# Two layers of linear attention and MLP on one core: the first tile's mean is taken ahead of its statistics, and the engines' lists are reordered

## The chip, the core and the metric

The kernel runs on one core of one Trainium2 chip. A core has five engines that run their own instruction streams and meet through semaphores: TensorE (PE in the profile; PEld is its weight load), VectorE (DVE), ScalarE (ACT), GpSimd (POOL) and SyncE (SP), which here only issues DMA transfers. TensorE writes to PSUM, a memory of eight banks; all other data lie in SBUF, 128 partitions wide. The metric is the time of one execution on the device, in microseconds (us). Smaller is better.

## The reference

`x` is 2048 tokens by 512 features in bf16. Four residual blocks follow each other: A, B, A, B, all with the same weights.

```python
def _A_ref(x, wqkv, wo):            # x is already layer-normed; H = 32 heads of 16
    q, k, v = split(x @ wqkv)
    phi = lambda t: jnp.where(t > 0, t + 1, jnp.exp(t)) + 1e-6
    pq, pk = phi(q), phi(k)
    kv = jnp.einsum("bhsd,bhse->bhde", pk, v)
    z = jnp.einsum("bhsd->bhd", pk)
    o = jnp.einsum("bhqd,bhde->bhqe", pq, kv) / (jnp.einsum("bhqd,bhd->bhq", pq, z)[..., None] + 1e-6)
    return merge(o) @ wo

def _B_ref(x, w1, b1, w2, b2):      # a layer norm of its own, 512 -> 1792 -> 512
    y = _layernorm(x)
    return gelu(y @ w1 + b1) @ w2 + b2

x = x + _A_ref(_layernorm(x), A_wqkv, A_wo)
x = x + _B_ref(_layernorm(x), B_w1, B_b1, B_w2, B_b2)     # and both once more
```

## The kernel before

Tokens are cut into 16 tiles of 128 (`st` = 0 to 15) and four chunks of four tiles (`c` = `st // 4`). Layer L (0 or 1) is one A block and one B block. All weights and the residual stay in SBUF.

A block. `norm` (L713) makes a normed tile `y` from `x`: statistics (`stats`, L741) and their aggregate (`aggr`, L743) on VectorE, variance plus epsilon (`veps`), its power -1/2 on GpSimd (`pow`, L756), and then centre and scale in one instruction (`norm`, L781 on VectorE, L776 on ScalarE). The four tiles of chunk 3, which is worked first (`C0=(3, 0, 1, 2)`), go another way: they are only centred (`cen`, L722), turned and projected, and the factor `rstd` is applied in the ScalarE instructions that read the projection (`exp`, `relu`, L848 and L859, with a scale from SBUF). The scaled `y` itself is made later (`ysc`, L766 and L763). A tile is turned (features onto partitions) either by TensorE with an identity matrix (`PT`, L823) and a ScalarE copy (`tc`, L833), or by a DMA transpose from SP (`TA`, `TB`, `TP`). `attn_k` (L869) and `attn_q` (L898) project it: `K0_12` is layer 0, tile 12; `Q0_3_1` is layer 0, chunk 3, tile 1 of the chunk. `phi` (L841) turns a projection into phi(k) or phi(q): `exp` and `relu` on ScalarE, `min` and a sum on VectorE (or GpSimd). `G` (L1004, L1036) sums y^T phi(k), so that v is never formed; `za` (L957) sums phi(k) over tiles; `KV`, `M` and `D` make from these the matrix that `WO` (L1152) multiplies phi(q) with, and its denominators.

B block. `mlp_front` norms and turns a tile (`TB`), `mlp_up` makes 14 groups of four matmuls `W1`L`_`c`_`ft (L1184, for chunk 0 in two halves of two tiles, last index 0 and 1) with a gelu each on ScalarE (L1190), `mlp_down` two groups of seven matmuls per tile (`W2`, last index 0 and 7, L1223), `RA` and `RB` are the residual sums on VectorE, and `b2`L`_`st adds the bias to the residual on VectorE or GpSimd.

Start. SP issues the loads: two tiles of chunk 3 (`x0`), the K and Q weights in two halves by rows (`wk0`, `wk1`), the other two tiles (`x2`), then the other chunks. TensorE runs 16 matmuls on constants (`warm`, L697) until the first tile is there. The first tile alone (`K_SPLIT=1`) is turned in two halves (`PTA0_12_0` and `PTA0_12_1`, L804, copied at L811), and its K and Q projections run in two halves, the first of which needs only `wk0` (L887, L917). `idle0_0` and `idle0_1` are two and one more matmuls on constants (`N_IDLE=[2, 1]`). The weights of V, the output projection and the MLP are loaded by six DMAs that GpSimd issues (`wv`, `wo`, `w1_0`, `w1_1`, `w2_0`, `w2_1`), the biases by SP (`b1`, `b2`).

Order. Nothing is ordered at run time. `CONF["ORDER"]` names for each engine every instruction in the order in which it runs; the program works out from the data which semaphores each has to wait for, and buffers and banks go to tiles as the lists' own estimate of time has them come free. `WAY` says which engine or which variant an instruction takes, `"normA0_5": "act"` for one.

Of the kernel before, what the change touches and what calls it, by code (L numbers as in the profile page):

```python
# [10 lines left out]
P = 128  # L11
# [271 lines left out]
def assign_waits(graph, order, sems, dma_sems):  # L283
# [10 lines left out]
    while len(done) < total:  # L294
        moved = False
        for e in ENGINES:
# [43 lines left out]
    N_WARM2=9, N_IDLE=[2, 1], XQ='sp', WKQ='sp sp', WK1=1, K_SPLIT=1, K_HALVES=(0, 1), X_HEAD=((0, 2), (2, 2)),  # L340
# [39 lines left out]
        "act":  # L380
# [164 lines left out]
def build_kernel(nc, A_x, A_wqkv, A_wo, B_x, B_w1, B_b1, B_w2, B_b2, out, conf=None, report=False):  # L545
# [5 lines left out]
    with ExitStack() as es:  # L551
# [161 lines left out]
        def norm(src, src_keys, src_tiles, double, on_act, prio, tag, src16=False, head=False):  # L713

            s = Tile(STATS, f"st{tag}")
            k = f"st{tag}"
            by_act = eng(f"st{tag}") == "act"
            centred = eng(f"cen{tag}") is not None

            def centre(mean, op):  # L720
                y = Tile(YB, f"y{tag}")
# [698 lines left out]
```

## Time and profile before

| | |
|---|---|
| time, median of 3 runs | 326.31 us (325.96 to 327.42) |
| time of the profiled execution | 326.6 us |
| its span, first to last instruction | 324.9 us |
| TensorE busy | 319.8 us, 98% of the span, 1703 matmuls |
| VectorE, ScalarE, GpSimd busy | 224.4, 193.7, 144.6 us |
| granted TensorE clock | 1.0 throughout |
| first DMA of x landed, first real matmul | 3.5 us, 5.34 us |
| last matmul started | 322.1 us |

The profiled execution is 1.7 us longer than its span, which is what lies ahead of the first and behind the last instruction. In the page, a row names the line, the engine, the operation, what it writes and reads, and the count; the bracket behind a row says how long the engine stood idle before it and what released it. The slices in tenths show how busy an engine was in each fortieth of the span. Ends of matmuls are modelled, so distances between starts are safer than busy times there.

### The profile page before, as it was taken

The page shows a single profiled execution, that of the slowest core. Times are in us where ns is not written, and L with a number is a line of the kernel's source. Part 1 is how long each engine was busy: PE and PEld are TensorE (multiplying, and loading weights), DVE is VectorE, ACT ScalarE, POOL GpSimd, SP SyncE. Part 2 cuts the span into 40 slices and gives each one's busy share as a digit, 9 for nine tenths or more (in the row PEclk, how much of TensorE's full clock was granted, in tenths as well). Part 3 has the DMA queues.
Part 4 walks back from the last instruction along what each step waited for, and adds up shares of the span by engine and source line. Part 5 has one row for each costly group of instructions (what it writes and reads, how often), then busy time and mean ns, then how long its engine had stood idle before and what let it go on. Part 6 is the DMA issues. An engine that isn't in the chain of part 4 may idle for free.

```text
span 324.9 us, 4758 instructions
## 1 busy us (share of the span) xinstructions
PE 319.8 (98%) x1703; PEld 157.9 (49%) x1703; DVE 224.4 (69%) x508; ACT 193.7 (60%) x333; POOL 144.6 (45%) x231
## 2 busy tenths in 40 slices
PE   7999999999999999999999999999999999999996
PEld 3444445567444444444444444558644444444443
DVE  4998979997998854003779999899899666100032
ACT  3999699745253235899527656978934734563300
POOL 4699476646522862500346825755904543100000
PEclk9999999999999999999999999999999999999999
DMA  7343179003331221210110300121230421300012
GB/s 259 144 64 72 40 236 355 18 16 76 40 64 35 58 57 32 43 22 17 34 33 16 67 17 0 18 48 36 41 72 18 82 65 50 81 0 15 31 65 69
DMA packets 46355, 20.37 MB, mean 63 GB/s; under 512 B 42044, under 2 KB 44220, under 8 KB 46332
## 3 DMA queue, kind: packets, MB, share of 16 engines
q1 hardware_dynamic: 45132, 15.32, 20.6%
q0 software_dynamic: 1056, 4.72, 4.1%
q8 instruction: 13, 0.21, 0.3%
q14 instruction: 10, 0.08, 0.1%
q10 hardware_dynamic: 144, 0.03, 0.0%
HBM read 8.00 MB, written 2.10 MB: 31 GB/s over the span
## 4 chain that ended last, share of the span: by engine, by line
PE 88%; DVE 4%; POOL 3%; DMA 2%; issue 1%; ACT 0%; SPq 0%
PE ps L1184 30%; PE ps L1223 29%; PE ps L1152 9%; PE ps L878 5%; PE ps L1036 4%; PE ps L908 4%; PE ps L1004 2%; PE ps L934 2%; DMA t<-in_A_x_dram 2%; DVE stats L741 1%; POOL rstd L756 1%; PE ps L1210 1%; PE ps L1128 1%; POOL zacc L957 1%; DVE yb L781 1%
## 5 line engine op out<-in xcount | busy, mean ns | idle before, releaser
L1190 ACT ACTIVATE gT<-ps,b1c 128x512 bf16<-128x512 f32 (+1 forms) x140 | 76.9, 600 | 70.9 <-PE ps L1184 70.6
L1184 PE MATMUL ps<-t,w 128*128 128x512 bf16 (+1 forms) x560 | 102.6, 336 | 0.0
L1223 PE MATMUL ps<-w,gT 128*128 128x512 bf16 x434 | 98.2, 379 | 0.0
L1184 PEld LDWEIGHTS ps<-t,w 128*128 128x128 bf16 x560 | 54.5, 98 | 43.9 <-ACT t L833 0.6
L1223 PEld LDWEIGHTS ps<-w,gT 128*128 128x128 bf16 x434 | 42.5, 98 | 50.5 <-ACT gT L1190 0.2
L848 ACT ACTIVATE eb<-ps 128x512 bf16<-128x512 f32 x56 | 32.8, 608 | 17.2 <-PE ps L878 10.6
L756 POOL TENSOR_TENSOR rstd<-veps,neghalf 128x1 f32<-128x1 f32 x64 | 38.7, 615 | 5.6 <-DVE veps L754 3.2
L1233 DVE TENSOR_TENSOR pkb<-ps,xsb 128x512 bf16<-128x512 f32 x15 | 10.0, 682 | 32.8 <-PE ps L1223 32.7
L741 DVE BATCH_NORM_STATS2 stats<-xsb 128x6 f32<-128x512 f32 x48 | 32.2, 681 | 0.2
L878 PE MATMUL ps<-wqkv,t 128*128 128x512 bf16 x124 | 31.2, 379 | 0.0
L1229 DVE TENSOR_TENSOR xsb<-ps,xsb 128x512 f32<-128x512 f32 x16 | 10.9, 686 | 29.2 <-PE ps L1223 29.2
L1152 PE MATMUL ps<-gtb,t 128*128 128x512 bf16 x128 | 30.7, 379 | 0.0
L754 POOL TENSOR_SCALAR veps<-mv 128x1 f32<-128x1 f32 x29 | 8.3, 297 | 39.1 <-DVE mv L743 38.4
L859 ACT ACTIVATE rb<-ps 128x512 bf16<-128x512 f32 x38 | 22.7, 612 | 2.0 <-PE ps L878 1.5
L776 ACT ACTIVATE yb<-xsb,nmr,rstd 128x512 bf16<-128x512 f32 x21 | 16.8, 812 | 10.8 <-POOL nmr L773 10.8
L781 DVE TENSOR_SCALAR yb<-xsb,mv,rstd 128x512 bf16<-128x512 f32 x27 | 15.3, 574 | 10.1 <-POOL rstd L756 9.9
L1169 POOL TENSOR_TENSOR xsb<-xsb,b2b 128x512 f32<-128x512 f32 x14 | 17.6, 1258 | 5.4 <-DVE yb L781 4.9
L1116 POOL TENSOR_TENSOR t<-t,rr 128x512 bf16<-128x512 bf16 x7 | 7.7, 1100 | 26.2 <-DVE rr L1112 16.5
L746 POOL TENSOR_SCALAR veps<-mv 128x1 f32<-128x1 f32 x32 | 10.2, 319 | 20.6 <-DVE mv L743 18.8
L1152 PEld LDWEIGHTS ps<-gtb,t 128*128 128x128 bf16 x128 | 12.4, 98 | 14.0
L908 PE MATMUL ps<-wqkv,t 128*128 128x512 bf16 x76 | 19.2, 379 | 0.0
L878 PEld LDWEIGHTS ps<-wqkv,t 128*128 128x128 bf16 x124 | 11.8, 98 | 14.5 <-ACT rb L859 0.6
(102 smaller groups left out, 415.9 us busy)
## 6 DMA issues: line engine op xcount, KB each, us to landing
w<-in_B_w_dram POOLq DMA_DIRECT2D x4, 896.0 KB, 7.2
out_dram<-pkb SPq DMA_DIRECT2D x15, 128.0 KB, 2.0
t<-in_A_x_dram SPq DMA_DIRECT2D x3, 512.0 KB, 7.3
wqkv<-in_A_wqkv_dram SPq DMA_DIRECT2D x2, 512.0 KB, 4.6
t<-yb SPq DMA_TRANSPOSE x56, 2.5
t<-in_A_x_dram SPq DMA_DIRECT2D x2, 256.0 KB, 4.2
wqkv<-in_A_wqkv_dram POOLq DMA_DIRECT2D x1, 512.0 KB, 4.4
wo<-in_A_wo_dram POOLq DMA_DIRECT2D x1, 512.0 KB, 5.1
```

Of the source, the lines that this page charges most:

```text
L741: G.op("dve", lambda e: e.bn_stats(stats[:, s.slot, :], src()), 602, reads=src_keys, writes=[k + "s"], tiles=[s, *src_tiles], prio=prio, n ...
L756: G.op("pool", lambda e: e.tensor_tensor(rstd[:, s.slot:s.slot + 1], veps[:, s.slot:s.slot + 1], neghalf[:], op=ALU.pow), 530, reads=[k + ...
L781: G.op("dve", lambda e: e.tensor_scalar(yb[:, y.slot, :], src(), stats[:, s.slot, 2:3] if by_act else mv[:, s.slot, 0:1], rstd[:, s.slot:s ...
L848: G.op("act", lambda e: e.activation(eb[:, et.slot, :], bank(bt), ACT.Exp, scale=factor()), 569 if by else 483, reads=[src_key, *more], wr ...
L859: G.op("act", lambda e: e.activation(rb[:, rt.slot, :], bank(bt), ACT.Relu, scale=factor()), 569 if by else 478, reads=[src_key, *more], w ...
L878: ins = e.matmul(bank(b), lhsT=yTa(yT)[:, dt, k * P:(k + 1) * P], rhs=wqkv[:, dt, D:2 * D], start=(dt == 0), stop=(dt == DT - 1))
L908: ins = e.matmul(bank(b), lhsT=yTa(yT)[:, dt, k * P:(k + 1) * P], rhs=wqkv[:, dt, 0:D], start=(dt == 0), stop=(dt == DT - 1))
L1152: ins = e.matmul(bank(wb), lhsT=yTa(pq)[:, kt, k * P:(k + 1) * P], rhs=gtb[:, kt, :], start=(kt == 0), stop=(kt == DT - 1))
L1169: G.op("pool" if on_pool else "dve", lambda e: e.tensor_tensor(xsb[:, st, :], xsb[:, st, :], b2b[:], op=ALU.add), 1120 if on_pool else 600 ...
L1184: ins = e.matmul(bank(b, n), lhsT=w1[:, dt, ft * P:(ft + 1) * P], rhs=yTa(yT)[:, dt, k0 * P:k1 * P], start=(dt == 0), stop=(dt == DT - 1))
L1190: G.op("act", lambda e, ft=ft, b=b, k0=k0, k1=k1, n=n: e.activation(gT[:, g.slot, ft * 512 + k0 * P:ft * 512 + k1 * P], bank(b, n), ACT.Ge ...
L1223: ins = e.matmul(bank(b), lhsT=gT[:, g.slot, ft * 512 + k * P:ft * 512 + (k + 1) * P], rhs=w2[:, ft, :], start=(ft == 0), stop=(ft == FT - 1))
```

## The change

Three things are done at the head, and all lists are written anew.

1. The first tile (12) and the second (13) no longer take the mean from `bn_stats`. For tile 12 ScalarE sums the second half of each row (an activation copy with an accumulator) while VectorE sums the first half (`redA0_12`, a reduction); `negA0_12` adds the two and multiplies by -1/512; the tile is centred in two halves (`cenA0_12_1`, then `cenA0_12_0`), and each half of its turn waits only for its half. For tile 13 ScalarE sums the whole row. The statistics follow behind the centring and serve only the variance.
2. `K_SPLIT` is 2: K and Q of tile 13 are projected in two halves too (its turn stays whole). `N_IDLE` is `[4, 1]`.
3. The lists of all five engines are new, over the whole kernel. The instructions themselves, apart from the above, are the same and run on the same engines.

```diff
-    N_WARM2=9, N_IDLE=[2, 1], XQ='sp', WKQ='sp sp', WK1=1, K_SPLIT=1, K_HALVES=(0, 1), X_HEAD=((0, 2), (2, 2)),
+    N_WARM2=9, N_IDLE=[4, 1], XQ='sp', WKQ='sp sp', WK1=1, K_SPLIT=2, K_HALVES=(0, 1), X_HEAD=((0, 2), (2, 2)),
...
         "pe":
-            "warm PTA0_12_0 PTA0_12_1 idle0_0 PTA0_13 idle0_1 K0_12_0 K0_12 Q0_3_0_0 Q0_3_0 K0_13 PTA0_14 Q0_3_1 "
-            "PTA0_15 K0_14 G0_12_0 K0_15 Q0_3_2 Q0_3_3 G0_13_0 PTA0_1 K0_0 G0_14_0 K0_1 G0_15_0 G0_0_0 K0_3 K0_2 "
...
+            "warm PTA0_12_0 PTA0_12_1 idle0_0 Q0_3_0_0 PTA0_13 Q0_3_0 idle0_1 K0_12_0 K0_12 K0_13_0 K0_13 Q0_3_1_0 "
+            "PTA0_14 PTA0_15 Q0_3_1 K0_14 K0_15 Q0_3_3 G0_12_0 Q0_3_2 G0_13_0 K0_0 PTA0_1 G0_14_0 K0_1 K0_3 G0_15_0 "
+            "K0_2 Q0_0_2 G0_0_0 Q0_0_3 Q0_0_0 G0_1_0 K0_8 G0_2_0 K0_4 G0_3_0 K0_6 K0_10 K0_5 Q0_0_1 K0_11 G0_4_0 K0_7 "
...
+            "W10_0_1_0 W10_0_0_0 W10_0_13_0 W10_0_8_0 W10_0_7_0 W10_0_11_0 W20_0_0 W10_0_9_0 W10_0_12_0 W20_1_0 "
+            "W20_1_7 W10_0_13_1 W10_0_7_1 W10_0_1_1 W10_0_6_1 W20_0_7 W10_0_3_1 W10_0_4_1 W10_0_5_1 W10_0_10_1 "
...
+            "W11_3_1_0 W11_3_7_0 W11_3_3_0 W11_3_0_0 W11_3_5_0 W11_3_9_0 W11_3_4_0 W21_5_0 W11_3_11_0 W11_3_6_0 "
+            "W21_5_7 W11_3_13_0 W11_3_10_0 W11_3_2_0 W21_7_7 W11_2_3_0 W11_2_7_0 W11_2_10_0 W11_2_2_0 W21_13_0 "
...
         "act":
-            "tcA0_12_0 tcA0_12_1 tcA0_13 reluk0_12 expk0_12 expq0_3_0 reluq0_3_0 tcA0_14 expk0_13 reluk0_13 tcA0_15 "
+            "sumA0_12 sumA0_13 tcA0_12_0 tcA0_12_1 tcA0_13 expq0_3_0 reluq0_3_0 reluk0_12 expk0_12 tcA0_14 tcA0_15 "
+            "reluk0_13 expk0_13 reluq0_3_1 expk0_14 reluk0_14 normA0_3 expq0_3_3 reluq0_3_3 expq0_3_1 expk0_15 tcA0_1 "
...
+            "gelu1_2_1_0 gelu1_2_6_0 gelu1_2_12_0 gelu1_2_11_0 gelu1_2_0_0 gelu1_2_5_0 gelu1_2_9_0 gelu1_2_13_0 "
...
         "dve":
-            "ones statsA0_12 statsA0_13 aggrA0_12 aggrA0_13 cenA0_12 cenA0_13 vepsA0_12 yscA0_13 yscA0_12 statsA0_14 "
...
+            "ones redA0_12 negA0_12 cenA0_12_1 cenA0_12_0 statsA0_12 negA0_13 aggrA0_12 cenA0_13 vepsA0_12 statsA0_13 "
+            "aggrA0_13 yscA0_12 statsA0_14 statsA0_15 aggrA0_14 aggrA0_15 cenA0_14 cenA0_15 statsA0_0 vepsA0_14 "
...
+            "phiq0_0_3 mink0_8 phiq0_3_0 normA0_11 phik0_8 mink0_4 phik0_4 mink0_6 phiq0_0_2 mink0_10 phik0_10 "
...
+            "cpm0_2 pz0_2_0 red0_2_0 RA0_0 statsB0_0 RA0_1 statsB0_1 aggrB0_0 aggrB0_1 RA0_3 RA0_2 normB0_1 pz0_3_1 "
+            "normB0_0 RA0_4 minq0_2_3 statsB0_3 RA0_5 pz0_3_0 statsB0_2 RA0_6 red0_3_1 aggrB0_2 RA0_7 aggrB0_3 "
+            "statsB0_7 red0_3_0 statsB0_5 minq0_2_2 normB0_2 den0_3_1 normB0_3 red0_3_2 den0_3_2 statsB0_4 minq0_2_1 "
...
+            "RB1_4 statsB1_10 aggrB1_10 normB1_10 b21_11 normB1_8 b21_13 b21_8 RB1_5 RB1_7 RB1_12 RB1_13 RB1_15_0 "
...
         "pool":
-            "powA0_4 nmrA0_7 powA0_9 powA0_6 nmrA0_6 nmrA0_9 za0_0 za0_1 vepsA0_11 powA0_11 za0_2 za0_3 phik0_6 w2_1 "
-            "phiq0_1_2 wv wo phiq0_1_1 w2_0 w1_1 w1_0 pr0_1_0 pr0_0_2 pr0_1_1 pr0_1_2 pr0_1_3 vepsB0_1 powB0_1 "
...
+            "nmrA0_7 vepsA0_11 vepsA0_9 powA0_11 powA0_9 za0_0 nmrA0_9 za0_1 za0_2 phik0_6 za0_3 eps6 phiq0_1_1 "
+            "phiq0_1_2 wo wv w2_0 w1_0 pr0_0_2 pr0_1_0 pr0_1_1 w1_1 w2_1 pr0_1_2 pr0_1_3 vepsB0_1 powB0_1 vepsB0_0 "
+            "powB0_0 phiq0_2_3 b20_0 vepsB0_2 powB0_2 pz0_3_2 vepsB0_3 powB0_3 vepsB0_7 vepsB0_6 vepsB0_5 vepsB0_4 "
...
         "sp":
-            "TB0_1 TB0_2 TB0_3 TP0_3_1 TP0_2_0 TB0_6 TB0_4 TB0_5 TB0_7 TP0_2_3 TP0_2_2 TP0_3_0 TP0_2_1 TP0_3_2 "
+            "TB0_1 b2 TB0_3 TB0_2 TP0_3_0 TP0_3_2 TB0_7 TB0_5 TB0_6 TB0_4 TP0_3_3 TP0_2_0 TP0_2_3 TP0_3_1 TP0_2_2 "
...
+            "TB1_12 TB1_13 TB1_15 OD2 TB1_9 TB1_10 TB1_11 TB1_8 OD13 OD12 OD4 OD1 OD15_0 OD14 OD0 OD6 OD9 OD5 OD10 "
...
+        "pz1_3_1": "dve", "pz1_3_2": "pool", "pz1_3_3": "pool", "stA0_12": "both", "stA0_13": "sum", "tc_10": "act", "tc_11": "dve",
...
+            early = eng(f"st{tag}") if eng(f"st{tag}") in ("both", "sum") else None
...
+                if early == "both":
+                    halves = cf["K_HALVES"]
+                    n = D // len(halves)
+                    G.parts[f"y{tag}"] = tuple(f"y{tag}_{h}" for h in halves)
+                    for h in halves:
+                        cs = slice(n * h, n * h + n)
+                        G.op("dve", lambda e, cs=cs: e.tensor_scalar(yb[:, y.slot, cs], src()[:, cs], mean(), None, op0=op), 180,
+                             reads=[k + "m", *src_keys], writes=[f"y{tag}_{h}"], tiles=[s, y, *src_tiles], prio=prio, name=f"cen{tag}_{h}", lat=40,
+                             fast=True)
+                    return y
...
+                h0 = D // 2 if early == "both" else 0
+                G.op("act", lambda e: e.activation(eb[:, et.slot, h0:D], src()[:, h0:D], ACT.Copy, accum_out=st6(0)), 450 if h0 else 630,
+                     reads=src_keys, writes=[k + "s"], tiles=[s, et, *src_tiles], prio=prio, name=f"sum{tag}", lat=90)
+                if h0:
+                    G.op("dve", lambda e: e.tensor_reduce(st6(3), src()[:, 0:h0], axis=mybir.AxisListType.X, op=ALU.add), 330, reads=src_keys,
+                         writes=[k + "t"], tiles=[s, *src_tiles], prio=prio, name=f"red{tag}", lat=40)
+                    G.op("dve", lambda e: e.tensor_scalar(st6(2), st6(0), st6(3), -1.0 / D, op0=ALU.add, op1=ALU.mult), 75,
+                         reads=[k + "s", k + "t"], writes=[k + "m"], tiles=[s], prio=prio, name=f"neg{tag}", lat=40)
...
+                y = centre(lambda: st6(2), ALU.add)
+                G.op("dve", lambda e: e.bn_stats(stats[:, s.slot, :], src()), 602, reads=src_keys, writes=[k + "s", k + "t", k + "m"],
+                     tiles=[s, *src_tiles], prio=prio, name=f"stats{tag}", lat=50)
...
-                    if f"yT{L}_{4 * c + k}" in G.parts:
+                    if L == 0 and c == HC and k < cf["K_SPLIT"]:
```

More of the change, by code (lines that the diff above doesn't have):

```diff
@@ L724, in centre @@
                 return y
-            if by_act:
+            if early:
+                et = Tile(EB, f"sq{tag}")
+                st6 = lambda i: stats[:, s.slot, i:i + 1]
+                h0 = D // 2 if early == "both" else 0
[6 more added lines that the diff above has]
+                         reads=[k + "s", k + "t"], writes=[k + "m"], tiles=[s], prio=prio, name=f"neg{tag}", lat=40)
+                else:
+                    G.op("dve", lambda e: e.tensor_scalar(st6(2), st6(0), -1.0 / D, None, op0=ALU.mult), 75,
+                         reads=[k + "s"], writes=[k + "m"], tiles=[s], prio=prio, name=f"neg{tag}", lat=40)
+                y = centre(lambda: st6(2), ALU.add)
+                G.op("dve", lambda e: e.bn_stats(stats[:, s.slot, :], src()), 602, reads=src_keys, writes=[k + "s", k + "t", k + "m"],
+                     tiles=[s, *src_tiles], prio=prio, name=f"stats{tag}", lat=50)
+                G.op("dve", lambda e: e.bn_aggr(mv[:, s.slot, :], stats[:, s.slot, :]), 92, reads=[k + "s"], writes=[k + "a"],
+                     tiles=[s], prio=prio, name=f"aggr{tag}", lat=55)
+                head = eng(f"veps{tag}") == "dve"
+                G.op("dve" if head else "pool",
+                     lambda e: e.tensor_scalar(veps[:, s.slot:s.slot + 1], mv[:, s.slot, 1:2], EPS, None, op0=ALU.add),
+                     75 if head else 182, reads=[k + "a"], writes=[k + "v"], tiles=[s], prio=prio, name=f"veps{tag}", lat=50)
+            elif by_act:
                 et = Tile(EB, f"sq{tag}")
@@ L763, in scaled @@
                         G.op("act", lambda e: e.activation(yb[:, y.slot, :], yb[:, y.slot, :], ACT.Copy, scale=rstd[:, s.slot:s.slot + 1]), 640,
-                             reads=[k + "r", f"y{tag}"], writes=[f"y{tag}"], tiles=[s, y], prio=prio, name=f"ysc{tag}", lat=90)
+                             reads=[k + "r", f"y{tag}"], writes=list(G.parts.get(f"y{tag}", (f"y{tag}",))), tiles=[s, y], prio=prio, name=f"ysc{tag}", lat=90)
                     else:
                         G.op(way, lambda e: e.tensor_scalar(yb[:, y.slot, :], yb[:, y.slot, :], rstd[:, s.slot:s.slot + 1], None, op0=ALU.mult),
-                             300 if way == "dve" else 1150, reads=[k + "r", f"y{tag}"], writes=[f"y{tag}"], tiles=[s, y], prio=prio,
+                             300 if way == "dve" else 1150, reads=[k + "r", f"y{tag}"],
+                             writes=list(G.parts.get(f"y{tag}", (f"y{tag}",))), tiles=[s, y], prio=prio,
                              name=f"ysc{tag}", lat=40, fast=way == "dve")
@@ L805, in turn @@
                         return ins
-                    o = G.op("pe", turn, n * 66, reads=[ykey, f"id{P}"], writes=[f"{key}_{h}p"], tiles=[bs[h], y], prio=prio, name=f"PT{tag}_{h}",
+                    o = G.op("pe", turn, n * 66, reads=[f"{ykey}_{h}" if ykey in G.parts else ykey, f"id{P}"], writes=[f"{key}_{h}p"], tiles=[bs[h], y], prio=prio, name=f"PT{tag}_{h}",
                              lat=MM_DRAIN, n=n)
@@ L919, in part @@
                                 return ins
-                            G.op("pe", part, n * MM, reads=[f"yT{L}_{4 * c + k}_{h}", f"wq_{h}"] + ([f"q{L}_{c}_{k}"] if i else []),
+                            G.op("pe", part, n * MM, reads=[f"yT{L}_{4 * c + k}" + (f"_{h}" if f"yT{L}_{4 * c + k}" in G.parts else ""), f"wq_{h}"] + ([f"q{L}_{c}_{k}"] if i else []),
                                  writes=[f"q{L}_{c}_{k}"], tiles=[b, yT], prio=prio + 0.8 * k,
```

246 rows, old and new, of tables (ORDER, WAY) are left out of this document.

## The prediction

> **What bounds the kernel now.** I read the busy slices first, then the table by stage, then TensorE's waits and its instructions in order of time, and last what the other engines did just ahead of those waits. Every engine runs its own list in the order written in the kernel, so the n-th row of an engine in the trace is the n-th name of its list; the names below are put to rows in that way.
>
> ```profile
> PE   7999999999999999999999999999999999999996
> 7.40:36.00 28.60, 27.87 (x136) 12.20 (x137) 26.91 (x76) 25.32 (x45) 21.53 (x42) 1.00 0.39 98
> 36.00:62.00 26.00, 26.00 (x172) 12.77 (x171) 23.66 (x53) 22.27 (x42) 16.25 (x18) 1.00 0.58 193
> 78.00:322.20 244.20, 244.20 (x1254) 118.92 (x1251) 155.53 (x335) 134.34 (x223) 93.49 (x146) 1.00 0.19 42
> ```
>
> In the stage rows the columns are the stage, its length, and the busy time of PE, PEld, DVE, ACT and POOL. TensorE is busy for the whole of every stage after the head, so the time is TensorE's work plus its waits. A shorter kernel can only come from waits, and these are all that there are:
>
> ```profile
> PE ps L697 <- PEq L1405: 0.8, 1, 0.8
> PE ps L1004 <- DVE pkb L854: 0.7, 1, 0.7
> PE ps L887 <- DMA wqkv<-in_A_wqkv_dram: 0.6, 1, 0.6
> PE ps L804 <- DVE yb L722: 0.4, 1, 0.4
> ```
>
> The page models a matmul's end late, so I count from start to start. The next rows give the pace: four matmuls from 7.83 to 8.69, 0.216 us each. From there: 8.69 + 0.86 = 9.55, but the next starts at 9.75 (0.20 lost); 33.16 + 0.86 = 34.02, but the next starts at 34.89 (0.87 lost). Four more gaps near 19.7, 25.0, 28.5 and 32.0 are 0.08, 0.07, 0.04 and 0.07 (0.26). From 36 to the end all gaps together are under 0.1. Ahead of that TensorE stood from 6.65 to 7.40 for the second half of the K and Q weights (0.74).
>
> ```profile
> 6.21 0.60 PE L887 MATMUL ps<-wqkv,t 128*128 128x512 bf16 x2
> 7.40 0.59 PE L887 MATMUL ps<-wqkv,t 128*128 128x512 bf16 x2 [0.58 <-DMA wqkv<-in_A_wqkv_dram]
> 7.83 1.03 PE L917 MATMUL ps<-wqkv,t 128*128 128x512 bf16 x4
> 8.69 1.03 PE L878 MATMUL ps<-wqkv,t 128*128 128x512 bf16 x4
> 9.75 0.40 PE L823 MATMUL ps<-idp,yb 128*128 128x128 bf16 x4
> ...
> 33.16 1.03 PE L878 MATMUL ps<-wqkv,t 128*128 128x512 bf16 x4
> 34.89 1.04 PE L1004 MATMUL ps<-pkb,yb 128*128 128x512 bf16 x4 [0.70 <-DVE pkb L854]
> ```
>
> So after 7.40 there are 1.33 us to win (0.4% of 326.6). Half a per cent (1.6 us) is about what a measurement of this kernel tells from no change.
>
> **The change, part by part.** Sums go against the profiled execution, 326.6 us (span 324.9 and 1.7 around it); the median of the runs shown is 326.3, so 0.3 is taken off at the end.
>
> First tile. Before: x lands at 3.50, statistics of two tiles 1.29, aggregates to 4.89, centring 0.34, first turn at 5.34. After: a half sum on ScalarE beside one on VectorE, a scaling, two half centrings. No row shows these. ScalarE's half sum lies between its 128x256 copy (0.38) and its 512-wide scaling in SBUF (0.82, L763); I take 0.45, nearer in size to the first. The half reduction lies between 0.15 (a one-column instruction) and 0.69 (statistics over twice the columns) and is covered by the sum at up to 0.45. The scaling is 0.15 as L754; a half centring lies between 0.15 and 0.34, I take 0.21, and 0.13 to the next. 3.52 + 0.45 + 0.04 + 0.15 + 0.03 + 0.34 = 4.53; the warm-up matmuls end at 4.73, so the first turn comes at about 4.75 (5.0 at the upper ends): 0.6 earlier. It is worth 0: the list lets only two matmuls of the first weight half (Q0_3_0_0, before K0_12_0) and the second tile's turn run ahead of a matmul that needs the second half, as before, and that half lands at 7.26 either way. ScalarE's two sums fall into its idle stretch before 5.77. The second tile's power moves from 6.0 to about 7.6, as its statistics now follow its centring; its first reader (reluk0_13) runs at 11.4, which hides it; without that cover it would cost 1.6. The two extra filler matmuls lie under the weights' wait; the one that moves behind it costs 0.06.
>
> 7.4 to 11.1. Behind the weights the new list has 12 matmuls and the filler before the third turn: 7.40 + 2.65 = 10.05, when its centring (9.69) is done: the 0.20 goes. Next late is the fourth turn, whose bank expk0_12 gives back: Q0_3_0 ends at 7.99, then four ScalarE instructions (three at a pitch of 0.57, the last 0.70) end at 10.4, and the turn waits from 10.27 to 10.48. Then two matmuls, and K0_14 at 11.1 against 11.07. Worth 0.
>
> To 62. The 0.87 comes from this:
>
> ```profile
> 31.70 2.38 POOL L957 TENSOR_TENSOR zacc<-zacc,pkb 128x512 f32<-128x512 f32 x2
> 32.19 0.81 DVE L852 TENSOR_SCALAR eb<-eb 128x512 bf16<-128x512 bf16 x1
> 32.92 1.31 DVE L781 TENSOR_SCALAR yb<-t,mv,rstd 128x512 bf16<-128x512 bf16 x1
> 34.15 0.68 DVE L854 SCALAR_TENSOR_TENSOR pkb<-ps,eb 128x512 bf16<-128x512 f32 x1
> ```
>
> Two VectorE instructions that elsewhere take 0.28 and 0.41 end just after POOL's long additions (to 34.08). The second (normA0_11) stood ahead of phik0_4 (L854), for which TensorE waited; its power had stood behind two additions on POOL. In the new lists that power is ahead of all four of these additions, normA0_11 ahead of phik0_8, and G0_4 behind five other TensorE groups. So -0.87, and -0.26 for the small gaps. What is late next are the K and Q groups that need one of four banks back, the kind that made the small gaps; I put back as much, 0.25 (between 0 and 0.87, one such collision).
> [...]
>
> Weights. On POOL w1_1 and w2_1 now stand behind three long products; pr0_1_1 ended at 53.66, so the issue comes at 52.9 with 0.8 won, and lands 7.25 later (its row) at 60.1, or 8.74 (w1_0's) at 61.6; the first MLP matmul comes at 61.5. Cost 0 (to 0.1). pr0_1_2, behind two issues of 0.74 and 1.14, still starts when its reciprocal ends.
>
> At 72. The second half of the first MLP chunk started at 74.58, 0.04 after its last DMA transpose landed (74.54). W20_0_7 is moved behind it, so TensorE is there 1.51 earlier, and 0.8 by the head: at 72.3. VectorE's list from normB0_0 (ends 60.0) to normB0_3 holds eleven instructions of 0.60, five short ones and two of 0.45: 68.3. (POOL's two powers and the product pz0_3_2 between them end at 67.5.) SP then issues TB0_3, TB0_2 1.31 later, which lands 2.45 after that: 72.1. On POOL b20_0 now waits for b2, moved behind TB0_1 on SP; at the 2.0 of other 128 KB transfers it lands at 62.2, at its own row's 4.5 at 64.7, and the turn then lands at 73.0. I take +0.15 (0 to 2.7: at the old rows' pace normB0_3 ends at 71.2).
>
> At 284. TB1_8 now stands last, its norm on VectorE behind b21_11, which waits for ScalarE's normB1_11. From W11_3_6_0: 1.03 to its end, gelu 0.7, norm 0.81, TB1_11's issue 1.3, landing 2.45: 6.35. TensorE's own list to the reader: 6.48. I take +0.1 (0 to 0.5, the size of ScalarE's one instruction). Elsewhere the reordered lists carry the same work; 0, between -0.06 and one more collision (0.87).
>
> Sum: 0.06 - 1.13 + 0.25 + 0.15 + 0.1 = -0.57. 326.6 - 0.6 = 326.0, and 325.7 for the median.
>
> **Rivals.** [...]
> Mild late transposes: the waits at 72 and 284 cost 0.8 and 0.5 in place of 0.25: 326.8, up to 327.8 with one collision on top. For it: both margins are 0.1 to 0.2.
> Slower: at 72 VectorE needs as long as before for normB0_3, and the wait is 2.7: 328.3. It decides from a normB0_3 later than 68.5, and passes half a per cent from 70.7. For it: in the old trace 11.2 us passed between normB0_0 and normB0_3. Against: the old list held more between them, a wait for POOL's product and power among it.
> Faster: all 1.33 goes and nothing new comes: 325.0; beyond half a per cent only if the transfers also land earlier than here.
>
> **How the numbers follow.** Mine 0.42 (325.2 to 326.2), lock redrawn 0.19, mild 0.18, slower 0.16, faster 0.05. The range 324.9 to 328.0 takes in all but the end of the faster case and most of the slower one. Lock redrawn and mild are within half a per cent, as is mine.
>
> **What would show it.** The first turn at about 4.75, but the weights' wait still ending at 7.4; a wait of some 0.2 near 10.4; G0_4 without a wait, normA0_11 near 0.4; at 72 the second half's first matmul within 0.2 of the landing of TB0_2; at 284 the same for TB1_8. I am wrong if the stage from 78 to 320 holds a wait of over 0.5, or if normB0_3 ends after 70.

## The result, and the profile after

The changed kernel takes 327.45 us (median of 20 runs; 326.96 to 328.76) against 326.37 us (20 runs; 325.96 to 327.42) before. The ratio is 1.0033, with a 95% interval of 1.0024 to 1.0042: 1.1 us slower, where 0.6 us faster was forecast. The time lies inside the range, but on the other side of no change. The prediction took half a per cent for the least change that can be told from none; with 20 runs of each the interval is 0.2% wide, so this loss of 0.3% is clear of it.

The profiled execution took 326.96 us, with a span of 325.2. Its waits of TensorE, in the columns engine, line, what was waited for, sum in us, times, longest:

```profile
PE ps L916 <- ACT rb L897: 1.3, 1, 1.3
PE ps L699 <- PEq L1443: 0.8, 1, 0.8
PE ps L955 <- DMA wqkv<-in_A_wqkv_dram: 0.8, 2, 0.5
PE ps L861 <- DVE veps L791: 0.2, 1, 0.2
```

The wait for VectorE's L854 (0.7), which stood in the same table before the change, is gone. In its place stands one of 1.3 for ScalarE's L897 (`relu`). TensorE's instructions in order of time show both places:

```profile
24.94 1.03 PE L1042 MATMUL ps<-pkb,yb 128*128 128x512 bf16 x4
27.22 1.04 PE L916 MATMUL ps<-wqkv,t 128*128 128x512 bf16 x4 [1.25 <-ACT rb L897]
...
34.22 1.03 PE L916 MATMUL ps<-wqkv,t 128*128 128x512 bf16 x4
35.09 1.03 PE L1042 MATMUL ps<-pkb,yb 128*128 128x512 bf16 x4
```

The row at 35.09 is G0_4_0: 34.22 + 0.86 = 35.08, so the 0.87 that it waited before is won. The row at 27.22 is K0_8: 24.94 + 0.86 = 25.80, so from start to start 1.42 are lost (the bracket counts from a modelled end). Read in the same way, with 0.216 us a matmul, this trace and a second one of the same kernel (below) give these gaps after the weights have landed, all of 0.03 and more counted:

| gap before | before | forecast | after | after, second trace |
|---|---|---|---|---|
| PTA0_14, PTA0_15 | 0.20 | 0.21 | 0.33 | 0.33 |
| K0_8 | 0.07 | | 1.42 | 1.45 |
| G0_4_0 | 0.87 | 0 | 0 | 0 |
| other small ones up to 62 | 0.22 | | 0.35 | 0.29 |
| first group of the second half of the first MLP chunk (new lists: W10_0_13_1), at 73 to 75 | 0.06 | 0.15 | 0 | 0.34 |
| W11_2_3_0, at 285 | 0 | 0.1 | 0 | 0 |
| sum | 1.42 | 0.7 | 2.10 | 2.41 |

(Rows two and four together had 0.25 in the forecast, which summed the gaps before to 1.33, since it left out the 0.03 and the 0.06 behind 36. 32 of the 1705 matmuls have no record in the new trace; each leaves a false gap of 0.216, which is taken out here. TensorE's busy time, 317.8, is too low for the same reason.) With the filler's 0.06 the gaps make the changed kernel 0.74 and 1.05 longer; the medians differ by 1.08. TensorE's last matmul starts only 0.31 and 0.77 later than in the trace of before, because the second half of the weights (`wk1`) happened to land earlier: at 6.86 and 6.99 in the traces of the changed kernel, at 7.26 in that of before. Gaps and landing together give 0.34 and 0.78.

Why K0_8 waited, from the same trace of the changed kernel, all engines in order of time (start, length, engine, line):

```profile
23.07 1.79 POOL L811 TENSOR_SCALAR nmr<-mv,rstd 128x1 f32<-128x1 f32 x2
...
23.35 0.39 DVE L903 TENSOR_TENSOR pkb<-eb,rb 128x512 bf16<-128x512 bf16 x1
23.66 0.41 DVE L819 TENSOR_SCALAR yb<-t,mv,rstd 128x512 bf16<-128x512 bf16 x1
23.98 0.42 DVE L903 TENSOR_TENSOR pkb<-eb,rb 128x512 bf16<-128x512 bf16 x1
24.31 0.42 DVE L903 TENSOR_TENSOR t<-eb,rb 128x512 bf16<-128x512 bf16 x1
...
24.90 0.81 ACT L814 ACTIVATE yb<-t,nmr,rstd 128x512 bf16<-128x512 bf16 x1 [1.50 <-POOL nmr L811]
...
25.62 1.06 ACT L886 ACTIVATE eb<-ps 128x512 bf16<-128x512 f32 x2
...
26.57 0.60 ACT L897 ACTIVATE rb<-ps 128x512 bf16<-128x512 f32 x1
```

Two one-column instructions on POOL (nmrA0_10 and nmrA0_6: minus the mean times `rstd`, which ScalarE's norm needs) take 1.79, the second of them 1.10, from 23.76 to 24.86, just past the end of VectorE's run (24.73). By a run I mean instructions that follow each other without a pause, here phik0_1, normA0_4, phik0_3 and phiq0_3_2. The same form takes 0.27 elsewhere (the median of its 28). ScalarE stands for 1.5 at normA0_6, which needs the result, and behind it in its list stand expk0_2, expq0_0_2 and reluq0_0_2. These three are evictions: they read a projection out of its bank of PSUM, and when its last reader has ended, the bank is free for another group. reluq0_0_2 ends at 27.17 and gives back the bank that K0_8 is to write; K0_8 starts at 27.22. In all five traces in which K0_8 waits, it starts 0.05 to 0.06 after reluq0_0_2 has ended. In the old list normA0_6 stood later, at 28.14, and waited 0.1.

### The profile page after: what moved, and what is told of

Read it like the earlier page. It is cut to its first block, busy times and chain, and to the rows that moved or that the text cites. A ratio compares the mean times of both kernels' runs of the same rounds, so it can differ in the third digit from the quotient of the medians.

```text
span 325.2 us, 4742 instructions
## 1 busy us (share of the span) xinstructions
PE 317.8 (98%) x1673; PEld 158.3 (49%) x1705; DVE 218.5 (67%) x512; ACT 200.0 (62%) x341; POOL 143.1 (44%) x231
## 4 chain that ended last, share of the span: by engine, by line
PE 90%; DVE 5%; DMA 2%; issue 1%; ACT 0%; SPq 0%; ACTq 0%
PE ps L1261 29%; PE ps L1222 28%; PE ps L916 8%; PE ps L1190 6%; PE ps L1074 4%; PE ps L946 4%; PE ps L1042 4%; PE ps L972 3%; DVE stats L778 2%; DMA t<-in_A_x_dram 2%; DVE xsb L1195 1%; PE ps L1248 1%; PE ps L1166 1%; DVE rd L1145 1%; PE ps L1097 1%
## 5 line engine op out<-in xcount | busy, mean ns | idle before, releaser
L793 POOL TENSOR_TENSOR rstd<-veps,neghalf 128x1 f32<-128x1 f32 x64 | 39.5, 624 | 7.0 <-DVE veps L760 2.5
L886 ACT ACTIVATE eb<-ps 128x512 bf16<-128x512 f32 x56 | 31.7, 604 | 11.7 <-PE ps L916 7.6
L1271 DVE TENSOR_TENSOR pkb<-ps,xsb 128x512 bf16<-128x512 f32 x15 | 10.1, 679 | 31.0 <-PE ps L1261 30.9
L916 PE MATMUL ps<-wqkv,t 128*128 128x512 bf16 x117 | 29.4, 379 | 1.5 <-ACT rb L897 1.3
L897 ACT ACTIVATE rb<-ps 128x512 bf16<-128x512 f32 x38 | 22.4, 610 | 5.5 <-PE ps L916 2.9
L890 DVE TENSOR_SCALAR eb<-eb 128x512 bf16<-128x512 bf16 x18 | 7.1, 397 | 24.8 <-ACT eb L886 24.7
L783 POOL TENSOR_SCALAR veps<-mv 128x1 f32<-128x1 f32 x32 | 7.5, 234 | 30.6 <-DVE mv L780 29.4
L791 POOL TENSOR_SCALAR veps<-mv 128x1 f32<-128x1 f32 x28 | 8.1, 295 | 25.6 <-DVE mv L780 25.0
L946 PE MATMUL ps<-wqkv,t 128*128 128x512 bf16 x70 | 18.0, 379 | 0.1
L1207 DVE TENSOR_TENSOR xsb<-xsb,b2b 128x512 f32<-128x512 f32 x18 | 12.6, 707 | 8.1 <-ACT yb L814 8.1
```

Source lines behind the costliest of these rows:

```text
L793: G.op("pool", lambda e: e.tensor_tensor(rstd[:, s.slot:s.slot + 1], veps[:, s.slot:s.slot + 1], neghalf[:], op=ALU.pow), 530, reads=[k + ...
L886: G.op("act", lambda e: e.activation(eb[:, et.slot, :], bank(bt), ACT.Exp, scale=factor()), 569 if by else 483, reads=[src_key, *more], wr ...
L897: G.op("act", lambda e: e.activation(rb[:, rt.slot, :], bank(bt), ACT.Relu, scale=factor()), 569 if by else 478, reads=[src_key, *more], w ...
L916: ins = e.matmul(bank(b), lhsT=yTa(yT)[:, dt, k * P:(k + 1) * P], rhs=wqkv[:, dt, D:2 * D], start=(dt == 0), stop=(dt == DT - 1))
L946: ins = e.matmul(bank(b), lhsT=yTa(yT)[:, dt, k * P:(k + 1) * P], rhs=wqkv[:, dt, 0:D], start=(dt == 0), stop=(dt == DT - 1))
```

## The experiments

Theories: the chain just read (POOL, ScalarE, bank, K0_8); against it the new head (the two sums on ScalarE push the first group back); and landings of transfers that vary from execution to execution. Ratios are to the kernel before, taken beside each run; its own median is 326.3 to 326.9 in most of these sets and 327.8 in the last one, so times of different sections are compared by their ratios.

### The changed kernel again

> The changed kernel as it is, once more, for a second trace. Chain theory (POOL's nmrA0_6 ends late, ScalarE stands at normA0_6 with the evictions behind it, and K0_8 gets no bank): the wait of TensorE before K0_8 is there again, 1.2 to 1.6 us, and the time is 327.3 to 327.6. Landing theory (the difference between the medians is when the input transfers land, which varies): the wait is well under 1 or somewhere else, and the landing of wk1 moves by some 0.4 from 6.86.

327.64 us, ratio 1.0040 (1.0023 to 1.0057). K0_8 waits 1.45. wk1 lands at 6.99. The wait comes with the kernel, not with the execution.

### The old statistics with the new lists

```diff
-        "stA0_12": "both", "stA0_13": "sum",
+        "stA0_13": "dve",
 act
-sumA0_12 sumA0_13 tcA0_12_0
+tcA0_12_0
 dve
-ones redA0_12 negA0_12 cenA0_12_1 cenA0_12_0 statsA0_12 negA0_13 aggrA0_12 cenA0_13 vepsA0_12 statsA0_13 aggrA0_13 yscA0_12
+ones statsA0_12 statsA0_13 aggrA0_12 aggrA0_13 cenA0_12 cenA0_13 vepsA0_12 yscA0_12
```

> The changed kernel's lists, filler and projections by halves, but the first two tiles' mean taken from bn_stats and bn_aggr and the first tile centred whole, as before. Chain theory: the lists do it; the wait before K0_8 stays, 327.3 to 327.5. Rival (the new head does it: two more instructions on ScalarE and four on VectorE push the first group back): 326.3 or less, and no wait before K0_8.

327.43 us, ratio 1.0028 (1.0017 to 1.0038), K0_8 waits 1.48:

```profile
25.11 1.03 PE L1042 MATMUL ps<-pkb,yb 128*128 128x512 bf16 x4
27.45 1.04 PE L916 MATMUL ps<-wqkv,t 128*128 128x512 bf16 x4 [1.31 <-ACT rb L897]
```

The lists carry the loss; the new statistics have no part in it. (`K_SPLIT` and the filler stay as in the changed kernel here, and no run changes them alone.)

### The new statistics with the old lists

```diff
-K_SPLIT=2, N_IDLE=[4, 1], the new lists
+K_SPLIT=1, N_IDLE=[2, 1], the lists of before, with:
 act
+sumA0_12 sumA0_13 at the front
 dve
+redA0_12 negA0_12 cenA0_12_1 cenA0_12_0 statsA0_12 negA0_13 aggrA0_12 cenA0_13 vepsA0_12 statsA0_13 aggrA0_13 yscA0_12 at the front, yscA0_13 ahead of mink0_13
 pool
+powA0_12 ahead of vepsA0_13
```

> The kernel before with the new statistics alone: half sums on ScalarE and VectorE, the first tile centred in halves, the sum for the second tile on ScalarE; K_SPLIT, the filler and the rest of the lists as before. First turn at 4.8 to 4.9 in place of 5.34, the second half of the first projection still starts 0.14 after wk1 has landed; 326.2 to 326.5 by the theory that the weights bound the head, 325.8 by the theory that the earlier first turn is worth its 0.5.

326.44 us, ratio 1.0005 (0.9997 to 1.0014). The first turn starts at 4.92, wk1 lands at 6.91, and the first matmul that needs it starts at 7.05. An earlier first turn is worth nothing here: the second half of the weights bounds the head.

### ScalarE's place for normA0_6

```diff
 act
-reluk0_3 normA0_6 expk0_2 expq0_0_2 reluq0_0_2 normA0_10
+reluk0_3 expk0_2 expq0_0_2 reluq0_0_2 normA0_6 normA0_10
```

> Only normA0_6 is moved, on ScalarE, from ahead of expk0_2 to behind reluq0_0_2. Chain theory: the three evictions no longer stand behind nmrA0_6; reluq0_0_2 ends at about 25.6 in place of 27.17, K0_8 starts at about 25.8, the wait of 1.4 falls to under 0.3, and the time is 326.1 to 326.4. Theory that the loss is spread over the later stages or lies in the landings: no change, 327.4.

327.13 us, ratio 1.0018 (1.0008 to 1.0027). K0_8 starts without any wait, as the chain theory has it, but the time is not the 326.1 to 326.4 expected: about 0.5 of the 1.45 is won (0.3 to 0.7, by which median or ratio of the changed kernel it is set against). TensorE's instructions of this run:

```profile
24.75 1.03 PE L1042 MATMUL ps<-pkb,yb 128*128 128x512 bf16 x4
25.62 1.03 PE L916 MATMUL ps<-wqkv,t 128*128 128x512 bf16 x4
...
29.24 1.04 PE L916 MATMUL ps<-wqkv,t 128*128 128x512 bf16 x4
30.70 1.04 PE L916 MATMUL ps<-wqkv,t 128*128 128x512 bf16 x4 [0.42 <-DVE pkb L892]
32.18 1.04 PE L916 MATMUL ps<-wqkv,t 128*128 128x512 bf16 x4 [0.44 <-DVE pkb L892]
```

K0_6, K0_10 and K0_5 (the last three rows) now wait 0.17, 0.60 and 0.62 by their starts, for VectorE. These waits had been hidden behind the one before K0_8. With 0.27 that appears before W10_0_3_0, all gaps sum to 2.17, against 2.10 and 2.41 in the two traces of the changed kernel. VectorE's rows ahead of them, and POOL's:

```profile
27.27 1.04 DVE L890 TENSOR_SCALAR eb<-eb 128x512 bf16<-128x512 bf16 x1 [0.64 <-ACT eb L886]
...
30.56 0.83 DVE L890 TENSOR_SCALAR eb<-eb 128x512 bf16<-128x512 bf16 x1
```

```profile
26.88 1.16 POOL L995 TENSOR_TENSOR zacc<-zacc,pkb 128x512 f32<-128x512 f32 x1
...
30.09 1.15 POOL L995 TENSOR_TENSOR zacc<-zacc,pkb 128x512 f32<-128x512 f32 x1
```

minq0_0_3 and mink0_4, 0.28 elsewhere, take 1.04 and 0.83 and end 0.27 and 0.15 after POOL's additions za0_15 (26.88 + 1.16) and za0_0 (30.09 + 1.15): the collision that stood before G0_4_0 in the old lists, at two new places.

### Is it the instruction or the place?

```diff
 pool
-powA0_6 nmrA0_10 nmrA0_6
+powA0_6 nmrA0_6 nmrA0_10
```

> Only POOL's nmrA0_6 is moved, ahead of nmrA0_10. Chain theory: nmrA0_6 ends at 23.4 to 23.8 in place of 24.86, normA0_6 starts 1.1 earlier, K0_8's wait falls to about 0.3, and the time is 326.3. nmrA0_10, now where nmrA0_6 was, takes about 1.1 if VectorE's run of short bf16 instructions is what stretched that place, and 0.3 to 0.4 if it was the instruction itself. Theory that ScalarE's list alone is too slow there: K0_8 still waits about 1.

326.97 us, ratio 1.0023 (1.0010 to 1.0036). nmrA0_6, now first, takes 0.71 and ends at 23.75; nmrA0_10, now in its place, takes 1.10. It is the place. K0_8 waits 0.40, near the 0.3 expected, and K0_10 and K0_5, no longer hidden, 0.28 and 0.60, so that 326.3 is missed as above.

```diff
 dve
-phik0_1 normA0_4 phik0_3 phiq0_3_2 mink0_2 statsA0_9 phik0_2
+phik0_1 normA0_4 statsA0_9 phik0_3 phiq0_3_2 mink0_2 phik0_2
```

> The changed kernel with one VectorE instruction moved: statsA0_9 out of its place behind mink0_2 into the run of short bf16 instructions, between normA0_4 and phik0_3. Lock theory (a run of such instructions with no gap holds GpSimd off): nmrA0_6 on POOL, which took 1.10 and ended 0.13 after the last of the run, ends during statsA0_9, at 24.0 to 24.5, and takes 0.3 to 0.7. Rival (POOL is slow there for a reason of its own): 1.1 and 24.8 to 25.0 as before. The time is of less interest here, since phik0_3 comes 0.7 later and holds expq0_0_2: 327.0 to 327.6.

326.86 us, ratio 1.0015 (1.0004 to 1.0026). With statsA0_9 in the middle of the run, the two POOL instructions take 1.12 together in place of 1.79:

```profile
23.69 1.12 POOL L811 TENSOR_SCALAR nmr<-mv,rstd 128x1 f32<-128x1 f32 x2
24.90 0.40 POOL L791 TENSOR_SCALAR veps<-mv 128x1 f32<-128x1 f32 x2
25.39 1.12 POOL L793 TENSOR_TENSOR rstd<-veps,neghalf 128x1 f32<-128x1 f32 x1
```

nmrA0_6 takes 0.43 in place of 1.10 and ends at 24.82, inside statsA0_9 (24.60 to 25.29). This execution runs 0.62 behind that of the changed kernel here, so that is 24.20 by the other's time, in the span expected. The power behind it, 0.57 in the other traces, takes 1.12: it meets the rest of the run. Even so this one move won 0.6 to 0.8 of the 1.1 to 1.2 lost, more than was expected of it (327.0 to 327.6). K0_8 still waits 0.78, but no wait of 0.6 appears before K0_10 and K0_5 here.

### Taking the next waits too

```diff
 act
-reluk0_3 normA0_6 expk0_2 expq0_0_2 reluq0_0_2 normA0_10 expq0_0_3
+reluk0_3 expk0_2 expq0_0_2 reluq0_0_2 expq0_0_3 normA0_6 normA0_10
 dve
-aggrA0_9 statsA0_11 minq0_0_3 aggrA0_11 minq0_0_2 phiq0_0_3 mink0_8 phiq0_3_0 normA0_11 phik0_8 mink0_4 phik0_4
+aggrA0_9 minq0_0_3 minq0_0_2 phiq0_0_3 statsA0_11 aggrA0_11 mink0_8 phik0_8 phiq0_3_0 mink0_4 phik0_4 normA0_11
```

> The changed kernel with normA0_6 behind reluq0_0_2 as in the run before, and beyond that the instructions that then came late taken out of POOL's way: expq0_0_3 ahead of normA0_6 on ScalarE, and on VectorE minq0_0_3, minq0_0_2 and phiq0_0_3 ahead of statsA0_11, phik0_8 straight behind mink0_8, mink0_4 and phik0_4 ahead of normA0_11. Masking theory (K0_10 and K0_5 waited 0.6 each since minq0_0_3 and mink0_4 stood behind za0_15 and za0_0): minq0_0_3 takes 0.3 in place of 1.04, the waits before K0_10 and K0_5 fall to under 0.3 together, and the time is 326.2 to 326.5. Rival (the DMA transposes at 1.31 each are the next bound): K0_5 and K0_11 still wait 0.6 or more together, and the time stays at 326.9 to 327.2.

327.30 us, ratio 1.0032 (1.0021 to 1.0042): nothing is won. The collisions are gone (minq0_0_3 0.25, mink0_4 0.29), and what TensorE waits for has changed:

```profile
30.57 1.02 PE L916 MATMUL ps<-wqkv,t 128*128 128x512 bf16 x4
31.89 1.02 PE L916 MATMUL ps<-wqkv,t 128*128 128x512 bf16 x4 [0.30 <-DMA t<-yb]
33.81 1.02 PE L916 MATMUL ps<-wqkv,t 128*128 128x512 bf16 x3 [0.90 <-DMA t<-yb]
```

K0_10 and K0_5 wait 0.46 and 1.06 for their DMA transposes (K0_5's third matmul has no record; 31.89 + 0.86 = 32.75, and it starts at 33.81). normA0_6 and those behind it had to give way on ScalarE for the evictions, SP issues a transpose every 1.3, and TA0_6, TA0_10 and TA0_5 land at 30.43, 31.75 and 33.67 (2.4, 2.5 and 3.1 after their issues). The rival was right in kind, though K0_10 waits and not the K0_11 that it named, and the time is just above its 326.9 to 327.2: behind the collisions lie the transposes. The sizes come from the slowest of eleven executions (328.39, wk1 landed at 7.72), so they are those of one trace and not of the median.

### The same wait in the kernel before

```diff
 dve
-phik0_10 mink0_4 normA0_11 phik0_4 phiq0_3_2
+phik0_10 mink0_4 phik0_4 normA0_11 phiq0_3_2
```

> The kernel before, with VectorE's normA0_11 moved behind phik0_4 and nothing else. Collision theory (the 0.87 that TensorE waits before G0_4_0 is normA0_11 standing behind POOL's long additions, and is won by taking it out of the way): phik0_4 ends at about 33.7, G0_4_0 starts at 34.0 without a wait, normA0_11 still takes over 0.8 where it now stands, and the time is 325.5. Masking theory (behind that wait others are hidden that come out as soon as it goes): 326.0 to 326.4.

325.63 us, ratio 0.9977 (0.9969 to 0.9986): faster than both kernels. TensorE's instructions:

```profile
32.08 0.81 PE L934 MATMUL ps<-t,wqkv 128*128 128x512 bf16 x3 [0.40 <-DVE pkb L854]
32.72 1.03 PE L878 MATMUL ps<-wqkv,t 128*128 128x512 bf16 x4
33.59 1.03 PE L1004 MATMUL ps<-pkb,yb 128*128 128x512 bf16 x4
34.45 1.03 PE L878 MATMUL ps<-wqkv,t 128*128 128x512 bf16 x4
35.60 1.04 PE L1004 MATMUL ps<-pkb,yb 128*128 128x512 bf16 x4
```

G0_4_0 (33.59) follows its predecessor at once; phik0_4 ended at 33.29. normA0_11 takes 0.59 behind it, less than the 0.8 expected, since za0_3 was over by 33.65. A wait of 0.29 appears before G0_5_0 (35.60), and one of 0.34 before Q0_0_1 in place of 0.07 (the row at 32.08 lacks its first record; wk1 landed at 6.56 here, so TensorE came sooner). All gaps of this trace sum to 0.96, which is 0.46 less than before; the medians differ by 0.7, with an interval of 0.5 to 1.0.

### The wait before the third turn

```diff
 dve, beyond the move above
-statsA0_14 statsA0_15 aggrA0_14 aggrA0_15 cenA0_14 vepsA0_14 statsA0_3 cenA0_15
+statsA0_14 aggrA0_14 cenA0_14 statsA0_15 aggrA0_15 cenA0_15 vepsA0_14 statsA0_3
```

> The kernel before with normA0_11 behind phik0_4 and, beyond that, on VectorE aggrA0_14 and cenA0_14 straight behind statsA0_14, and cenA0_15 ahead of statsA0_3. If the 0.20 before PTA0_14 is a loss of its own, cenA0_14 ends at 8.4 to 8.8, the third turn starts without a wait, and the time falls by a further 0.2, to 325.4. If it is masked, K0_14 or PTA0_15 waits as long, and it stays at 325.6.

327.10 us against 326.94 for the kernel before beside it, ratio 0.9990 (0.9973 to 1.0008): inconclusive. In the trace x0 landed at 4.40 instead of 3.5, TensorE's head was late for that reason, and the wait before PTA0_14 that the edit aims at does not occur. The move of the section above is in this edit too, so its gain is not seen a second time here: the kernel before spreads from 325.91 to 328.33 in this set, and the intervals of the two ratios overlap.

### The kernel before again, and a late x0

> The kernel before as it is, for a second trace. If the landing of wk1 only varies from execution to execution, it lands anywhere between 6.5 and 7.7 here as in the others, TensorE's first matmul of that half starts 0.14 later, and the 0.87 before G0_4_0 is there again whatever the landing. If the order of the lists sets it, it lands within 0.1 of 7.26.

327.49 us, ratio to itself 1.0012 (0.9993 to 1.0031), beside the run above. wk1 lands at 7.03, 0.23 away from the first trace, and G0_4_0 waits 0.86 again. x0 lands at 4.18, and something else shows, in TensorE's instructions:

```profile
6.02 0.61 PE L804 MATMUL ps<-idp,yb 128*128 128x128 bf16 x4 [1.08 <-DVE yb L722]
...
7.16 1.91 PE L887 MATMUL ps<-wqkv,t 128*128 128x512 bf16 x4
8.87 1.22 PE L917 MATMUL ps<-wqkv,t 128*128 128x512 bf16 x4
9.93 1.03 PE L878 MATMUL ps<-wqkv,t 128*128 128x512 bf16 x4
```

The four matmuls from 7.16 take (8.87 - 7.16) / 4 = 0.43 each, twice 0.216, and the full pace comes within the next four, at about 9.3. In the first trace it comes at about 5.7, during the turns; until then the pace is half in both traces, from the first warm-up matmul on (0.43 from start to start). TensorE had stood 1.08 before its first turn here, against 0.40 in the first trace. So I delayed x0, with the old and with the new statistics:

```diff
 sp, in the kernel before and in the one with the new statistics and the old lists
-x0 wk0 wk1
+wk0 x0 wk1
```

> The kernel before with the first tile pair x0 issued behind the first half of the weights on SP, so that it lands about 1 later than 3.5. Theory that a pause of TensorE of about 1 or more before the first turn brings half rate back (0.43 a 512-column matmul): the first turn comes at 6.2 to 7.0, matmuls run at 0.43 up to about 10, and the time is 327.2 to 328.2. Rival (only the landing itself counts): matmuls run at 0.216 as soon as they start, and the time is 326.3 to 326.9.

> The same late x0, with the new statistics in place of the old (otherwise the lists of the kernel before). Theory that the earlier first turn is worth something only when x0 lands late: the first turn comes 0.4 to 0.6 earlier than in the run beside this one, the half rate ends that much earlier or doesn't come, and the time is 0.4 to 1.0 below that run's. Rival (the weights bound the head here too): the two are within 0.2.

329.34 us, ratio 1.0058 (1.0038 to 1.0078), and 329.44 us, ratio 1.0059 (1.0039 to 1.0078), beside a kernel before of 327.79. x0 lands at 5.92 and 5.71, later than meant. The first turn comes at 7.76 and at 7.07, and both run a stretch at half pace. First the old, then the new statistics, TensorE's instructions:

```profile
8.71 1.91 PE L887 MATMUL ps<-wqkv,t 128*128 128x512 bf16 x4
10.42 1.53 PE L917 MATMUL ps<-wqkv,t 128*128 128x512 bf16 x4
11.78 1.03 PE L878 MATMUL ps<-wqkv,t 128*128 128x512 bf16 x4
```

```profile
8.25 0.40 PE L861 MATMUL ps<-idp,yb 128*128 128x128 bf16 x4 [0.67 <-DVE veps L760]
...
8.54 1.42 PE L925 MATMUL ps<-wqkv,t 128*128 128x512 bf16 x4
9.76 1.91 PE L955 MATMUL ps<-wqkv,t 128*128 128x512 bf16 x4
11.46 1.52 PE L916 MATMUL ps<-wqkv,t 128*128 128x512 bf16 x4
```

Here the pace was full when the first turn came (its four matmuls take 0.24 and 0.23 from their start to that of the next row, against 0.40 in the trace above) and fell to half behind it. The profile's own clock shows it. The columns are the stretch, its length, the busy time of PE, PEld, DVE, ACT and POOL, then the granted clock, followed by two on DMA; first the old, then the new statistics:

```profile
9.10:10.10 1.00, 1.00 (x4) 0.41 (x3) 1.00 (x4) 0.34 (x1) 0.00 (x0) 0.50 1.04 426
11.10:12.10 1.00, 1.00 (x4) 0.39 (x3) 1.00 (x5) 0.56 (x2) 0.55 (x1) 0.50 0.04 16
```

By the distances between starts the half pace runs from about 8.0 to 11.4 with the old statistics, and from about 9.0 to 12.5 with the new ones. So half pace comes back as expected, after pauses of 2.92 and 2.13, and the time is beyond the 327.2 to 328.2 expected. But the earlier first turn is worth nothing here either: the second tile's centring now stands behind the first tile's statistics, so TensorE waits 0.67 again before PTA0_13, and the half pace sets in later and ends later. Of the changed kernel itself with a late x0 there is no trace.

## Why the prediction was wrong, point by point

The step that failed is the last clause on the stage up to 62: "What is late next are the K and Q groups that need one of four banks back, the kind that made the small gaps; I put back as much, 0.25 (between 0 and 0.87, one such collision)." The kind was right, the size was not: K0_8 waits 1.42, more than the upper end. I bounded a bank's wait by one delayed VectorE instruction in TensorE's own path. What happened is two engines longer: VectorE's run held POOL (1.10 for 0.27), POOL held ScalarE at an instruction for a tile not needed until K0_6 (ScalarE idle 1.5), and three evictions of other tiles stood behind it. In the old list normA0_6 stood behind expk0_2, expq0_0_3, reluq0_0_0 and expk0_8; in the new one it stands ahead of all four. That could be read in the order; the prediction has no word on it, nor on ScalarE's waits for POOL, and "Elsewhere the reordered lists carry the same work" covered them. Moving normA0_6 back behind the three evictions takes K0_8's wait away; that this wins only about 0.5 is the second thing that the clause left out, waits that stand hidden behind the first.

The same step saw the collision in one direction only, POOL's additions delaying VectorE. Here VectorE's run delayed POOL.

- G0_4_0: right. The 0.87 goes in the changed kernel, and the same 0.87 goes by moving one VectorE instruction in the old one (0.7 in the median). Six TensorE groups, not five, stand between K0_4 and it in the new list.
- The first tile worth 0: right. The first turn came at 4.80 (4.75 forecast), and the statistics alone gave 1.0005. Single terms were off: the half sum is a 0.42 row and a 0.19 row behind it that reads the accumulator, 0.51 together against 0.45; the scaling 0.21 against 0.15; a half centring 0.29 against 0.21.
- The weights' wait ended at 7.00, not 7.4, because wk1 landed at 6.86; the first matmul came 0.14 after the landing, as before.
- The fourth turn waits for expk0_12's bank, 0.33 against 0.21.
- At 72: right within its range. VectorE's list took 8.25 from the end of normB0_0 to that of normB0_3 (8.3 forecast), but all of it came some 1.1 later, TensorE too: normB0_3 ended at 69.45 (68.3 forecast; from 68.5 on it was to decide). W10_0_13_1 started at 73.39, 0.14 after TB0_2 had landed (73.25), which was also the end of the group ahead of it, so it waited 0; in the second trace 0.34.
- At 284: TB1_8 landed at 285.10, its reader started at 285.33 without a wait (0.1 forecast; the terms given there add up to 6.29, not 6.35). MLP weights: the last landed at 62.10 (61.6 at the latest in the forecast), without a wait of TensorE.
- No wait over 0.5 between 78 and 320: right.

Of the rivals, "lock redrawn" (0.19: the 0.87 comes back elsewhere, 326.6) was right in kind: a collision between VectorE and POOL is there again, at a new place. That a lock is behind it was the author's estimate, and no run shows one; the traces show a delayed instruction that ends just after the other engine's work (normA0_11 0.15 after POOL's addition, nmrA0_6 0.13 after VectorE's run). 326.6 was too low a price: a collision can cost more than the one that it replaces (1.42 here in place of 0.87), when it catches an engine with others queued behind. "Mild late transposes" had the time, 326.8 to 327.8, by a cause that gives at most 0.34 of it. That the time lies inside the range at all is luck: the upper part of the range was there for late transposes, not for a chain over POOL and ScalarE.

## What to carry to other kernels

A wait in TensorE's list is the surface of a stack: under the 1.4 before K0_8 lay 1.4 for VectorE (0.17, 0.60, 0.62), and under that as much for the transposes (0.08, 0.46, 1.06, in one trace), and taking the first away alone won about 0.5. When lists are reordered, look on each engine for an instruction that waits for another engine and is placed ahead of evictions that free a bank, and price its wait with the longest row of the engine it waits for (1.10 for nmrA0_6), not the shortest (0.25 for the same form). A single move (normA0_11 behind phik0_4) that let only small waits grow, 0.07 to 0.34 and 0 to 0.29, beat a whole new order.

## What the runs showed of the hardware that was not expected

A one-column POOL instruction took 0.27 in the median, 1.10 behind the rest of a run of VectorE's bf16 instructions in SBUF, 1.30 when that run was one instruction longer (mink0_2 joined it in the experiment with normA0_6 moved, and nmrA0_6 ended at 24.91, 0.13 after it), and 0.43 when statsA0_9 stood in the run. These instructions overlap (starts 0.32 apart, 0.41 long), and in these traces the POOL instruction in nmrA0_6's place ended just after the run (24.86 against 24.73 in the changed kernel, 24.83 against 24.69 with nmrA0_10 there) or during the statistics instruction (24.82, statsA0_9 from 24.60 to 25.29). The other way round a single VectorE instruction, normA0_11, took 1.31 in place of 0.41 and ended 0.15 after POOL's addition (34.23 against 34.08). What holds the one engine while the other works, no run shows.

In these traces TensorE runs at half pace from its first matmul on (0.43 a matmul of 512 columns from start to start, against 0.216 later). With a pause of 0.40 between the warm-up matmuls and the first turn the full pace came at about 5.7, with 1.08 at about 9.3, and with 1.30 (the trace of the wait before the third turn) at about 10.1. With pauses of 2.92 and 2.13 the pace had been full by the first turn, fell back to half and was full again at about 11.4 and 12.5. The granted clock shows the second kind (0.50 in the rows above) but not the first: it says 1.00 from the start in the first trace and in the second one of the same kernel. What sets the pace, no run shows. The full pace comes 3.5 later in the one trace of the kernel before than in the other (5.74 and 9.27), and each stretch of half pace with a late x0 is about 3.4 long (8.0 to 11.4, 9.0 to 12.5).

The second half of the weights, with the order of the loads unchanged, landed anywhere from 6.56 to 7.72 in twelve traces, and x0 from 3.44 to 4.40. That is about as much as the change did to the time, so a trace's end can be compared only after its landings have been.
